# Order of four row products on TensorE in a gated scan kernel: value, gate, gate, value instead of value, gate, value, gate

## Chip, cores and metric

One core of one Trainium2 chip. The metric is the device time of the whole program in microseconds (us), the median of several executions. An execution's time is some 1.7 us above the span of its trace (from the first to the last instruction); both are used below, each under its name.

Engines in the profile: PE is TensorE, PEld its weight loads, DVE is VectorE, ACT is ScalarE, POOL is GpSimd, SP is SyncE.

## The reference, cut to what matters

```python
# x: 8 x 4224 x 192; a causal convolution of 7 taps, one set of weights per group of 24 channels
x = conv(x, softmax(weight))
proj = x @ w_in                       # 192 -> 1024
val, gate = proj[..., :512], proj[..., 512:]
a = exp(A_log)                        # one decay per channel of 512 in the kernel
for t in range(S):                    # along the sequence, per batch
    h = a * h + val[:, t]
    ys[:, t] = h
out = (gate * sigmoid(gate) * ys) @ w_out     # 512 -> 192
```

(The sequential part is a scan; the reference takes the decay as drawn, between 0 and 0.61.) The depth of `x @ w_in` is 192, which is 128 rows and 64 rows of the array. So each value or gate product needs a full product and a row product of 64 rows.

## The kernel before

The sequence is cut into blocks of 960 positions; a step is one block and one of four groups of 128 channels, 144 steps in all. A pass of the main loop does two steps, s and s+1, and has the work of four engines in flight: TensorE makes value, gate, output and convolution products; DVE scans the value; ACT makes SiLU of the gate; POOL multiplies the two.

```python
ps_v = ctx.enter_context(tc.tile_pool(name="ps_v", bufs=2, space=bass.MemoryType.PSUM))
ps_m = ctx.enter_context(tc.tile_pool(name="ps_m", bufs=2, space=bass.MemoryType.PSUM))
# ... (cut) two tiles each, of two banks a tile. ps_v holds values, ps_m everything else.

def proj(ps, s, gate, full, start):
    # ... (cut) two instructions, one for each half of the 960 columns
    for k in range(2):
        o = ps[:, BANK - w + k * w : BANK + k * w].rearrange("p (t m) -> p t m", m=M)
        if full:
            nc.tensor.matmul(o, w1[:, m], cols(xc, k * nh, nh), ...)          # 128 rows
        else:
            r = slice(k * P // 2, k * P // 2 + P // 2)
            nc.tensor.matmul(o, w2[r, m], cols(xc, 2 * nh, nh, r), ...)       # rows 0-63 or 64-127
# ...
for p in range(NP):
    s = 2 * p
    b = s // NC
    scan(s)                               # DVE, reads the value of s
    if p:
        val(s + 1, True, True)            # (step, full or row product, first of its sum)
    gate(s, True, True)
    val(s + 1, False, False)
    gate(s, False, False)
    val(s + 2, False, True)
    gate(s + 1, False, True)
    silu(s)                               # ACT
    mul(nc.gpsimd, s)                     # POOL
    # ... (loads)
    gate(s + 1, True, False)
    val(s + 2, True, False)
    silu(s + 1)
    if p < NP - 1:
        scan(s + 1)
        mul(nc.gpsimd, s + 1)
    # ... (loads)
    late = 0 if b >= NSB - 7 else 2
    if LEAD <= p < NP - 2 and done_step(u) < s - late:
        units(1)                          # sixteen output products; need POOL's product of done_step(u)
    # ... (transposes, convolution products of a later block)
```

Three things matter. The two row instructions of a pair use different halves of the array and run side by side (in the trace they start 3 ns apart). The value of step s+2 goes into the tile that the scan of step s reads, as there are only two. And an output unit needs a product of POOL that is at least three steps back, but from block 29 on (`late = 0`) only one.

## Time and profile before

| | before |
|---|---|
| median time | 332.81 us (3 runs, 332.68 to 332.9) |
| span of the trace | 331.5 us |
| busy share of the span: PE, DVE, POOL, ACT | 96, 94, 95, 80% |

The groups that carry three of the engines, from the page of the kernel before (line, engine, operation, output and inputs, shapes, count; then busy us and mean ns; then the idle time in front and what ended most of it):

```profile
L487 POOL TENSOR_TENSOR y<-sg,h 128x960 bf16<-128x960 bf16 (+3 forms) x159 | 279.7, 1789 | 5.2 <-ACT sg L449 4.3
L464 DVE TENSOR_TENSOR_SCAN h<-av,h,pv 128x960 bf16<-128x960 f32 (+5 forms) x140 | 265.9, 1937 | 6.3 <-issue 2.7
...
L429 PE MATMUL pv<-xc,w 64*128 64x480 bf16 (+2 forms) x288 | 53.8, 365 | 2.5 <-DVE h L464 1.6
```

POOL's products and DVE's scans fill the two engines nearly alone. The last line is the value's row products: PE stands before them and the scan ends the wait. That 1.6 us is far less than what the wait costs, since idle time is counted from the modelled end of the product before, 0.38 us after its start, while the next could have started after 0.20. For this wait one has to read starts.

### The profile page before, as it was taken

The page shows a single profiled execution, that of the slowest core. Times are in us where ns is not written, and L with a number is a line of the kernel's source. Part 1 is how long each engine was busy: PE and PEld are TensorE (multiplying, and loading weights), DVE is VectorE, ACT ScalarE, POOL GpSimd, SP SyncE. Part 2 cuts the span into 40 slices and gives each one's busy share as a digit, 9 for nine tenths or more (in the row PEclk, how much of TensorE's full clock was granted, in tenths as well). Part 3 has the DMA queues.
Part 4 walks back from the last instruction along what each step waited for, and adds up shares of the span by engine and source line. Part 5 has one row for each costly group of instructions (what it writes and reads, how often), then busy time and mean ns, then how long its engine had stood idle before and what let it go on. Part 6 is the DMA issues. An engine that isn't in the chain of part 4 may idle for free.

```text
span 331.5 us, 6839 instructions
## 1 busy us (share of the span) xinstructions
PE 318.4 (96%) x2593; PEld 191.3 (58%) x2593; DVE 310.0 (94%) x190; ACT 264.6 (80%) x449; POOL 313.9 (95%) x210
## 2 busy tenths in 40 slices
PE   8888899999999999999999999999999999999984
PEld 3544446666555666666555566666555666665554
DVE  3699999999999999999999999999999999999991
ACT  4588888888888888888888888888888888887663
POOL 5699999999999999999999999999999999989992
PEclk9999999999999999999999999999999999999998
DMA  7589699989989698959696989799998999653223
GB/s 164 57 91 104 71 132 227 169 185 161 220 140 239 126 224 141 218 126 222 146 202 172 145 222 143 202 153 228 135 245 114 200 191 184 130 155 122 96 98 142
DMA packets 99512, 53.40 MB, mean 161 GB/s; under 512 B 89915, under 2 KB 90967, under 8 KB 99479
## 3 DMA queue, kind: packets, MB, share of 16 engines
q1 hardware_dynamic: 58375, 38.93, 50.0%
q0 software_dynamic: 40560, 13.55, 39.0%
q10 hardware_dynamic: 544, 0.49, 0.5%
q8 instruction: 20, 0.33, 0.4%
q14 instruction: 13, 0.11, 0.1%
HBM read 28.46 MB, written 25.95 MB: 164 GB/s over the span
## 4 chain that ended last, share of the span: by engine, by line
PE 85%; DMA 5%; ACT 4%; POOL 2%; DVE 1%; issue 1%; DVEq 0%; ACTq 0%
PE pm L496 25%; PE pm L423 18%; PE pv L423 16%; PE pv L429 12%; PE pm L429 8%; PE pm L254 6%; ACT sg L449 2%; DMA w2r<-in_moe_w_in_dram 2%; DMA xb<-in_x_dram 2%; ACT xc L102 1%; DVE h L464 1%; DMA xr<-in_x_dram 1%; POOL y L487 1%; DMA out_dram<-osb 1%; ACT yc L102 0%
## 5 line engine op out<-in xcount | busy, mean ns | idle before, releaser
L487 POOL TENSOR_TENSOR y<-sg,h 128x960 bf16<-128x960 bf16 (+3 forms) x159 | 279.7, 1789 | 5.2 <-ACT sg L449 4.3
L464 DVE TENSOR_TENSOR_SCAN h<-av,h,pv 128x960 bf16<-128x960 f32 (+5 forms) x140 | 265.9, 1937 | 6.3 <-issue 2.7
L449 ACT ACTIVATE sg<-pm 128x960 bf16<-128x960 f32 (+2 forms) x144 | 135.9, 954 | 39.2 <-PE pm L429 32.2
L496 PEld LDWEIGHTS <-y 128*128 128x128 bf16 x1056 | 91.0, 114 | 13.1 <-POOL y L487 0.6
L496 PE MATMUL pm<-wout,y 128*128 128x192 bf16 x1056 | 97.8, 246 | 0.7 <-POOL y L487 0.4
L423 PEld LDWEIGHTS <-w 128*128 128x128 bf16 x576 | 48.9, 97 | 61.5 <-issue 33.1
L423 PE MATMUL pm<-xc,w 128*128 128x480 bf16 (+2 forms) x288 | 81.3, 364 | 2.0 <-ACT xc L102 1.3
L423 PE MATMUL pv<-xc,w 128*128 128x480 bf16 (+2 forms) x288 | 80.8, 361 | 0.6 <-DVE h L464 0.4
L102 ACT COPY osb<-pm 128x384 f32<-128x384 f32 x131 | 62.7, 479 | 15.5 <-PE pm L496 13.5
L102 ACT CAST yc<-pm 128x256 bf16<-128x256 f32 (+2 forms) x140 | 59.7, 491 | 2.6 <-PE pm L254 2.6
L429 PE MATMUL pv<-xc,w 64*128 64x480 bf16 (+2 forms) x288 | 53.8, 365 | 2.5 <-DVE h L464 1.6
L429 PEld LDWEIGHTS <-w 64*128 64x128 bf16 x576 | 23.3, 94 | 50.8 <-issue 37.9
L429 PE MATMUL pm<-xc,w 64*128 64x480 bf16 (+2 forms) x288 | 52.5, 358 | 0.0
L464 DVE TENSOR_TENSOR_SCAN h<-av,pv 128x720 bf16<-128x720 f32 (+4 forms) x32 | 42.4, 1330 | 2.0 <-PE pv L429 2.0
L254 PE MATMUL pm<-xb,tb 126*128 126x192 bf16 (+1 forms) x280 | 34.0, 244 | 1.4 <-ACT sg L449 0.7
L254 PEld LDWEIGHTS <-tb 126*128 126x128 bf16 x288 | 24.6, 97 | 3.3 <-DMA xb<-in_x_dram 1.5
L128 POOL DMA_DIRECT2D xb<-in_x_dram x21 | 25.5, 1214 | 0.1
L194 PE MATMUL pm<-wm 128*128 128x512 bf16 x24 | 7.7, 480 | 1.3 <-DVE wm L138 1.3
L102 ACT COPY xc<-pm 128x960 bf16<-128x960 bf16 (+2 forms) x9 | 6.1, 728 | 0.6 <-PE pm L375 0.5
L194 PEld LDWEIGHTS <-wm 128*128 128x128 bf16 x24 | 2.7, 119 | 4.9 <-issue 2.7
L394 POOL CAST w<-w1r 128x512 bf16<-128x512 f32 x2 | 1.2, 606 | 3.7 <-DMA xsf<-in_x_dram 3.7
L375 PEld LDWEIGHTS <-yc 120*128 120x128 bf16 x57 | 3.4, 98 | 1.3 <-ACT yc L102 0.6
(59 smaller groups left out, 30.2 us busy)
## 6 DMA issues: line engine op xcount, KB each, us to landing
out_dram<-osb SPq DMA_DIRECT2D x65, 384.0 KB
xb<-in_x_dram POOLq DMA_DIRECT2D x13, 756.0 KB, 12.4
xb<-in_x_dram POOLq DMA_DIRECT2D x7, 378.0 KB, 5.6
xb<-in_x_dram POOLq DMA_DIRECT2D x1, 519.8 KB, 9.8
xc<-yc SPq DMA_TRANSPOSE x31
w1r<-in_moe_w_in_dram SPq DMA_DIRECT2D x1, 448.0 KB
xr<-in_x_dram ACTq DMA_DIRECT2D x1, 283.5 KB
w2r<-in_moe_w_in_dram SPq DMA_DIRECT2D x2, 128.0 KB
```

Source lines behind the costliest of these rows:

```text
L102: return eng.copy(o, i) if eng is nc.scalar else eng.tensor_copy(o, i)
L128: nc.gpsimd.dma_start(xt[:, a0 : a0 + n, :], rows(FIRST[b0], n))
L194: nc.tensor.matmul(pw[:, 0:BANK], wm[:, 0:P], wm, start=True, stop=True)
L254: nc.tensor.matmul(pc[:, :, i * G : i * G + G], tb[:, h, :], xt[:, a0 : a0 + n, h * G : h * G + G], start=True, stop=True, skip_group_chec ...
L375: nc.tensor.transpose(pt[:, o + i * M : o + i * M + M], y[0:M, k * P : k * P + P], ident)
L394: nc.gpsimd.tensor_copy(w1[:, lo : lo + DI], w1r[:, lo : lo + DI])
L423: nc.tensor.matmul(o, w1[:, m], cols(xc, k * nh, nh), start=start, stop=not start, skip_group_check=True,)
L429: nc.tensor.matmul(o, w2[r, m], cols(xc, 2 * nh, nh, r), start=start, stop=not start, skip_group_check=True,)
L449: nc.scalar.activation(sg[:, 0 : 2 * w], pgs.pop(s)[:, BANK - w : BANK + w], Act.Silu)
L464: nc.vector.tensor_tensor_scan(h[:, lo:hi], av[:, c : c + 1].to_broadcast([P, hi - lo]), pv[:, BANK - w + lo : BANK - w + hi], initial=0.0 ...
L487: eng.tensor_mul(yr[c][:, ring(t0 + lo, hi - lo)], sg[:, lo:hi], h[:, lo:hi])
L496: nc.tensor.matmul(ps[:, o : o + D], yr[c][:, r.start + j : r.stop : UB], wout[:, c, :], start=(c == 0 and j % 2 == 0), stop=(c == NC - 1) ...
```

## The change

Its intent: the value of step s+2 is the one row product of the four that waits for a scan. Putting the gate's in front of it gives the scan one slot more. No product is added or removed.

```diff
         gate(s, True, True)
         val(s + 1, False, False)
         gate(s, False, False)
+        gate(s + 1, False, True)
         val(s + 2, False, True)
-        gate(s + 1, False, True)
         silu(s)
```

## The prediction

> **Names.** One pass of the main loop handles two steps. V1 and V2 are the value products of steps s+1 and s+2, G0 and G1 the gate products of s and s+1. Each consists of two full products (128 rows) and a pair of row products (64 rows each, the two running side by side). TensorE's order in a pass is: V1 full, G0 full, the four row pairs V1 G0 V2 G1, G1 full, V2 full, sixteen output products, four convolution products. The change makes the row pairs V1 G0 G1 V2.
>
> **What bounds the kernel now.** First the page: busy shares and the chain that ended last.
>
> ```profile
> PE 318.4 (96%) x2593; PEld 191.3 (58%) x2593; DVE 310.0 (94%) x190; ACT 264.6 (80%) x449; POOL 313.9 (95%) x210
> ...
> PE 85%; DMA 5%; ACT 4%; POOL 2%; DVE 1%; issue 1%; DVEq 0%; ACTq 0%
> ```
>
> Three engines are nearly full, so no share names the bound, and the chain names PE only because PE is followed whenever it shows no gap. So I went to the timeline of PE, start to start, over two passes (columns: start, time, engine, line, operation, tiles, shapes, count):
>
> ```profile
> 152.93 0.57 PE L423 MATMUL pv<-xc,w 128*128 128x480 bf16 x2
> ...
> 154.05 0.36 PE L429 MATMUL pm<-xc,w 64*128 64x480 bf16 x2
> 154.25 0.37 PE L429 MATMUL pv<-xc,w 64*128 64x480 bf16 x2
> ...
> 157.23 0.57 PE L423 MATMUL pv<-xc,w 128*128 128x480 bf16 x2
> ...
> 158.13 0.38 PE L429 MATMUL pv<-xc,w 64*128 64x480 bf16 x2
> 158.35 0.37 PE L429 MATMUL pm<-xc,w 64*128 64x480 bf16 x2
> 158.69 0.38 PE L429 MATMUL pv<-xc,w 64*128 64x480 bf16 x2
> 158.89 0.38 PE L429 MATMUL pm<-xc,w 64*128 64x480 bf16 x2
> ```
>
> The first pass takes 157.23 - 152.93 = 4.30 us and its row pairs start 0.20 apart. In the second, V2's pair starts 0.34 after G0's: PE stood for 0.14 us. Next pass starts at 161.67, so this one took 4.44. The scans say what it stood for:
>
> ```profile
> 152.00 2.19 DVE L464 TENSOR_TENSOR_SCAN h<-av,h,pv 128x960 bf16<-128x960 f32 x1
> ...
> 154.31 2.21 DVE L464 TENSOR_TENSOR_SCAN h<-av,h,pv 128x960 bf16<-128x960 f32 x1
> ...
> 156.44 2.19 DVE L464 TENSOR_TENSOR_SCAN h<-av,h,pv 128x960 bf16<-128x960 f32 x1
> ```
>
> The scan from 156.44 ends at 158.63 and V2's pair starts at 158.69: V2 needs the value buffer (two of them) that this scan reads. DVE stands too: the first scan ends at 154.19, the next starts at 154.31, because its V1 row pair only began at 153.84. Two engines wait for each other in turn. Third, POOL, by stretches (us, then PE, PEld, DVE, ACT, POOL busy), then at single gaps (idle before and what ended it in brackets), then PE's wait for it:
>
> ```profile
> 60.00:177.00 117.00, 116.55 (x958) 70.87 (x957) 115.40 (x67) 97.31 (x166) 116.85 (x70) 1.00 1.02 182
> 177.00:280.00 103.00, 102.42 (x843) 62.89 (x842) 101.45 (x56) 86.10 (x145) 100.53 (x60) 1.00 1.01 178
> ```
>
> ```profile
> 195.28 2.01 POOL L487 TENSOR_TENSOR y<-sg,h 128x960 bf16<-128x960 bf16 x1 [0.69 <-ACT sg L449]
> ...
> 212.80 2.01 POOL L487 TENSOR_TENSOR y<-sg,h 128x960 bf16<-128x960 bf16 x1 [0.43 <-ACT sg L449]
> ```
>
> ```profile
> 279.63 1.01 PE L496 MATMUL pm<-wout,y 128*128 128x192 bf16 x10 [0.40 <-POOL y L487]
> ```
>
> POOL is full to 177 us, working off a backlog: its product of step 15 starts 4.6 us after scan and SiLU are there, that of step 74 only 0.1 us after. Then small gaps appear. The last line shows PE waiting for POOL in pass 60, where the kernel's rule for emitting output units loosens and a unit needs the step just before.
>
> **What the Trainium skill says.** "TensorE: Matmul & The Clock Gate", Part 3, The mechanism: matrix products stay in program order, only weight loads are pulled ahead. The trace agrees: G1, whose inputs are there, starts 0.20 us behind V2 at 158.89, not before it. "TensorEngine Tiling (Array Packing)", Key Properties: changing the tiling mode drains the array. The trace agrees: the last row pair lasts 0.29 to 0.30 us to the next full product's start against 0.20 inside the group, and full to row costs as much. Both orders switch twice a pass, so this cost stays. "Perfetto Trace Analysis", Identifying the Most-Contended Engine: matmul busy time is a poor measure of PE and occupancy a good one for VectorE and GpSimd; here PE's 96% includes the stand of 0.14 us, so it agrees.
>
> **The change part by part.** Nothing is removed or added; DVE, ACT, POOL and SyncE keep their lists word for word. On PE two pairs change places, and V2's wait for the scan goes with it.
>
> *The loop it shortens.* Take it over two passes: scan end to V2's pair 0.06 us; V2's pair to the next pass's V1 pair 3.89 (V2 rows 0.20, G1 rows 0.31, G1 full 0.41, V2 full 0.41, output 1.32, convolution 0.33, V1 full 0.41, G0 full 0.50); V1's pair to the start of its scan 0.47; then two scans, 2.13 start to start plus 2.19. Sum 8.74 us, and the passes measure 4.30 + 4.44 = 8.74: this loop sets the pace. Moving G1's rows ahead of V2's takes one slot, 0.20, out of it: 8.54. PE's own work is twice 4.30 = 8.59, so now PE sets the pace, without V2 waiting, and two passes gain 0.15 us. In passes whose scan is cut at a sequence border the scans are 0.04 longer each; there some 0.03 of wait remains.
>
> *Sum over the run.* V2's slot over 0.20 adds up, in the timeline, to 2.02 us in 26 passes from 74 to 187 us, 0.48 in three to 200, 1.26 in 17 to 275, 0.04 in the first of the next seven: 3.8 us of PE time before pass 60. The 1.4 us before 74 follow mostly single late scans (0.59 at 57.98) that the order doesn't touch. After pass 60, six passes hold 0.47 us.
>
> *What POOL lets through.* POOL's continuous pace is 4.28 us a pass (steps 15 to 74, loads included) and PE's would be 4.30, so POOL keeps its backlog of about 4 us instead of losing it. It can win only its gaps: from 177 us to the product of step 119, which pass 60 needs, 2.4 us, of which 0.3 is a load behind a memset and likely stays. That product ended at 279.57 and should end near 277.4. PE would arrive at 278.57 - 3.8 = 274.8 and wait some 2.5 us for it. So of PE's 3.8 us some 2.0 pass through pass 60. Behind it POOL has no loads and runs at 3.95 a pass, faster than PE, so the rest is PE's and the scans': I allow 0.3 of the 0.47, as passes without convolution are bound by two scans, 4.26. Total 2.3 us: 332.8 - 2.3 = 330.5 us.
>
> **The rivals.** *Everything passes:* if POOL had no say, the 3.8 + 0.47 us would all show: 328.5 us. For: POOL's gaps after 177 show that it was waiting. Against: it has none in the 117 us before, and PE waits for it in pass 60. *G1 takes the wait:* G1 now comes 0.20 us earlier and needs a buffer that ACT is emptying:
>
> ```profile
> 153.17 0.93 ACT L102 CAST yc<-pm 128x256 bf16<-128x256 f32 x3
> ```
>
> These casts end at 154.10; with the 0.06 to 0.09 us that releases take here, G1 could start by 154.19, and its new place is 154.25. Margin 0.06 in passes with three casts, more in the others (one cast, end 158.28, place 158.55). If it fails, V2 stands behind it too: half the gain gone, 331.8 us. *Nothing moves:* scans are the true bound with 2 x 2.13 = 4.26 us a pass of 4.37; or POOL's first 177 us fix the end: 332.8 us. Against: DVE stands 0.04 to 0.13 us in each pass, and POOL's late gaps are real. *Output waits for SiLU:* the first output product needs SiLU(s), which ends 0.09 before it at 155.49 in the pass without a wait; that path is as long as PE's, unchanged by the order, and I give it little.
>
> **Range and chances.** The centre is 330.5 us. Most of the uncertainty is how many of POOL's gaps close and whether pass 60 swallows more: 329.3 if half of the held-back gain gets out, 332.2 if G1's wait or new gaps eat most of it. The three runs before spread only 0.22 us. Over 2% faster would be under 326.2, beyond even the first rival: 0.01. Over 2% slower has no mechanism here: 0.01. Within 2%: 0.98.
>
> **What would show it.** V2's slot excess gone (each pass near 4.30 us between 74 and 270 us); DVE's stand before the odd scans smaller or moved; POOL without gaps to step 119, its backlog near 4 us there; PE's wait for POOL in pass 60 grown from 0.6 to about 2.5 us; scans 3 to 4 us earlier at 270 us, but the end only some 2 us. I am wrong if a new wait stands before G1's row pair, if POOL's backlog empties all the same, or if the pace stays at 4.37.

## The result, and the profile after

| | before | after | ratio |
|---|---|---|---|
| first series | 332.75 us (4 runs) | 329.27 us (4 runs, 329.21 to 330.65) | 0.9907 (0.988 to 0.9933) |
| second series, on one chip | 332.65 us (11 runs) | 329.80 us (6 runs, 329.15 to 330.79) | 0.9917 (0.9894 to 0.994) |

A ratio is the mean time of one kernel's runs over that of the other's runs of the same rounds, with its 95% interval, so not quite the ratio of the medians beside it. The gain is 0.8 to 0.9%: 2.9 to 3.5 us by the medians.

The page of the changed kernel, busy shares and chain:

```profile
PE 314.1 (96%) x2593; PEld 198.3 (61%) x2593; DVE 308.7 (94%) x190; ACT 262.5 (80%) x449; POOL 313.4 (96%) x210
...
PE 82%; DMA 5%; ACT 4%; POOL 4%; DVE 2%; issue 1%; DVEq 0%; ACTq 0%; POOLq 0%
```

Busy shares hardly move and would not have told anything. What moved is in the timeline of PE, here one pass and the start of the next:

```profile
154.70 0.57 PE L423 MATMUL pv<-xc,w 128*128 128x480 bf16 x2
155.11 0.57 PE L423 MATMUL pm<-xc,w 128*128 128x480 bf16 x2
155.61 0.38 PE L429 MATMUL pv<-xc,w 64*128 64x480 bf16 x2
155.82 0.57 PE L429 MATMUL pm<-xc,w 64*128 64x480 bf16 x4
156.22 0.37 PE L429 MATMUL pv<-xc,w 64*128 64x480 bf16 x2
156.52 0.58 PE L423 MATMUL pm<-xc,w 128*128 128x480 bf16 x2
...
159.00 0.57 PE L423 MATMUL pv<-xc,w 128*128 128x480 bf16 x2
```

The two gate pairs are one row now (four instructions in the same tile pool). V2 starts at 156.22, 0.40 after the first of them, two slots of 0.20, and the pass takes 159.00 - 154.70 = 4.30 us. So does the next, which begins at 159.00 and ends at 163.29. The pass of 4.44 us is gone. In the 26 passes between 74 and 187 us the stands of V2 added up to 2.02 us before. Now, from pass 12 to 66, the slot before V2 exceeds 0.20 only at the sequence borders, by 0.02, and once at a late scan, by 0.29 (the pass from 184.81).

DVE and POOL by stretches (us, then busy PE, PEld, DVE, ACT, POOL); the first fence is the kernel before, in a stretch that the prediction did not show, the second the changed one:

```profile
177.00:264.00 87.00, 86.82 (x716) 53.49 (x715) 85.65 (x48) 73.12 (x124) 85.25 (x50) 1.00 1.02 175
```

```profile
60.00:177.00 117.00, 116.81 (x976) 75.69 (x974) 116.99 (x67) 98.72 (x171) 116.87 (x70) 1.00 1.02 183
177.00:264.00 87.00, 86.87 (x727) 56.44 (x728) 86.66 (x50) 73.19 (x126) 86.89 (x50) 1.00 0.95 183
```

POOL stood for 1.75 us of these 87 us; now it stands for 0.11. DVE, which stood 1.60 us in the 117 us before, has no gap left there, but it is not full by its own work: its scans now start 2.13 and 2.17 us after one another in turn, 4.30 us for two, PE's pace.

Then pass 60 of the changed kernel, the output products:

```profile
273.77 0.49 PE L496 MATMUL pm<-wout,y 128*128 128x192 bf16 x4
...
274.67 0.36 PE L496 MATMUL pm<-wout,y 128*128 128x192 bf16 x2 [0.41 <-POOL y L487]
...
276.61 1.01 PE L496 MATMUL pm<-wout,y 128*128 128x192 bf16 x10 [1.59 <-POOL y L487]
...
277.46 0.49 PE L254 MATMUL pm<-xb,tb 126*128 126x192 bf16 x4
```

Four products run, then two, then ten: each group needs POOL's product of one more step, and the last group starts when that of step 119 is there. The sixteen take 3.70 us to the start of the next row instead of 1.32, a wait of 2.38 us. Before it was 0.59.

By stretches, with the start of each pass taken from PE's timeline:

| stretch of the span | before, us | after, us | gained |
|---|---|---|---|
| start to pass 7 | 42.46 | 42.02 | 0.44 |
| passes 7 to 11 | 22.88 | 22.38 | 0.50 |
| passes 12 to 59 | 210.53 | 206.72 | 3.81 |
| pass 60 | 4.94 | 6.68 | -1.74 |
| passes 61 to 66 | 25.97 | 25.45 | 0.52 |
| pass 67 to the end | 24.68 | 24.33 | 0.35 |
| span | 331.46 | 327.58 | 3.88 |

The first row is for the most part not the order's: POOL's first product started at 15.66 and 15.13 us, and what it waits for (the weights' transfer and cast) lies ahead of every product that moved. In the other runs that start lies between 14.7 and 15.7 us, below 15.0 with both orders. Pass 7 began between 41.6 and 42.5 us with the orders that wait and between 41.4 and 42.0 with the changed one (runs with chained scan pieces left out), so a small part of the 0.44 may be the order's; no run separates it.

### The profile page after: what moved, and what is told of

Read it like the earlier page. It is cut to its first block, busy times and chain, and to the rows that moved or that the text cites. A ratio compares the mean times of both kernels' runs of the same rounds, so it can differ in the third digit from the quotient of the medians.

```text
span 327.6 us, 6839 instructions
## 1 busy us (share of the span) xinstructions
PE 314.1 (96%) x2593; PEld 198.3 (61%) x2593; DVE 308.7 (94%) x190; ACT 262.5 (80%) x449; POOL 313.4 (96%) x210
## 4 chain that ended last, share of the span: by engine, by line
PE 82%; DMA 5%; ACT 4%; POOL 4%; DVE 2%; issue 1%; DVEq 0%; ACTq 0%; POOLq 0%
PE pm L496 25%; PE pm L423 18%; PE pv L423 15%; PE pv L429 11%; PE pm L429 7%; PE pm L254 6%; POOL y L487 3%; ACT sg L449 2%; DVE h L464 2%; DMA xb<-in_x_dram 2%; DMA w2r<-in_moe_w_in_dram 2%; ACT xc L102 1%; DMA xr<-in_x_dram 1%; DMA out_dram<-osb 1%; ACT yc L102 0%
## 5 line engine op out<-in xcount | busy, mean ns | idle before, releaser
L449 ACT ACTIVATE sg<-pm 128x960 bf16<-128x960 f32 (+2 forms) x144 | 133.9, 954 | 36.1 <-PE pm L429 31.5
L429 PEld LDWEIGHTS <-w 64*128 64x128 bf16 x576 | 30.4, 94 | 47.5 <-issue 31.3
L429 PE MATMUL pm<-xc,w 64*128 64x480 bf16 (+2 forms) x288 | 40.6, 358 | 0.5 <-ACT xc L102 0.5
```

The costliest lines, as they stand in the source:

```text
L429: nc.tensor.matmul(o, w2[r, m], cols(xc, 2 * nh, nh, r), start=start, stop=not start, skip_group_check=True,)
L449: nc.scalar.activation(sg[:, 0 : 2 * w], pgs.pop(s)[:, BANK - w : BANK + w], Act.Silu)
```

## The experiments

V1, V2, G0, G1 are the row pairs as in the prediction. For the pace I give the time of passes 12 to 59 from each trace, as in the table.

### Where V1 and V2 stand

If the way from V2's pair to the next pass's V1 pair sets the pace, then V1 counts as much as V2. Two more orders test it: one with V2 last but V1 late, one with V2 third and V1 late.

```diff
-        val(s + 1, False, False)
         gate(s, False, False)
+        val(s + 1, False, False)
         gate(s + 1, False, True)
         val(s + 2, False, True)
```

> Row pairs in the order G0 V1 G1 V2: V2 stays last as in the changed kernel, but V1 comes one slot (0.20 us) later. Loop theory (the way from V2's pair to the next V1's pair and two scans set the pace): that way is 3.89 us again as in the kernel before, so 8.74 us for two passes, 4.37 a pass; V2 waits for the scan again; 332.8 us (332.2 to 333.4). Rival 'V2 only has to be last': 329.3 us, passes of 4.30. Rival 'two gate products side by side run better on the array': no adjacent gates here, 332.8 us too, but then without a wait of V2 and with longer slots of the row pairs.

Measured: 331.99 us, ratio 0.9978 (0.9946 to 1.0009). Passes 12 to 59 took 210.44 us, against 210.53 of the kernel before. In its timeline V2 waits just as before, though it is last:

```profile
157.72 0.37 PE L429 MATMUL pv<-xc,w 64*128 64x480 bf16 x2
157.93 0.36 PE L429 MATMUL pm<-xc,w 64*128 64x480 bf16 x2
158.26 0.38 PE L429 MATMUL pv<-xc,w 64*128 64x480 bf16 x2
```

V2 starts 0.33 after G1 instead of 0.20. The time is 0.2 us below the band that I gave, the pace is right to a tenth of a microsecond. "V2 only has to be last" falls. The rival of the adjacent gates named the same time, but with longer slots and without a wait of V2; the slots are 0.20 as ever and the wait is there.

```diff
-        val(s + 1, False, False)
         gate(s, False, False)
-        gate(s + 1, False, True)
+        val(s + 1, False, False)
         val(s + 2, False, True)
+        gate(s + 1, False, True)
```

(against the changed kernel)

> Row pairs in the order G0 V1 V2 G1: V2 third as in the kernel before, V1 one slot later. Loop theory: the way from V2 to the next V1 grows to 4.09 us, the loop to 8.94, 4.47 us a pass, 0.10 more than before in some 53 passes less the wait in pass 60: 337.5 us (336.5 to 338.5), slower than both kernels. Rival 'only V2's place in the group counts': 332.8 us. Rival 'like products side by side run better': 329.3 us.

Measured: 338.22 us, ratio 1.0174 (1.0145 to 1.0203). Passes 12 to 59 took 215.19 us, 4.48 each, where 4.47 was expected:

```profile
106.48 0.37 PE L429 MATMUL pv<-xc,w 64*128 64x480 bf16 x2
107.01 0.38 PE L429 MATMUL pv<-xc,w 64*128 64x480 bf16 x2 [0.17 <-DVE h L464]
107.22 0.38 PE L429 MATMUL pm<-xc,w 64*128 64x480 bf16 x2
```

V2 stands 0.53 after V1, a wait of 0.33, twice and more that of the kernel before. Four orders of the same instructions, and only the number of slots from V2 to the next V1 tells their pace: one less is 206.7 us, the same is 210.5 and 210.4, one more is 215.2. Both rivals fall with this one, as they expected no loss.

### Longer scans, first attempt

A loop through two scans must answer to their length. Every uncut scan was cut in two, in both orders.

```diff
-        ends = sorted(set([0] + cuts + [n]))
+        ends = sorted(set([0] + cuts + [n] + ([] if cuts else [n // 3])))
```

> The kernel before, with every uncut scan cut into two (a third and two thirds), which makes a scan some 0.04 us longer; result unchanged. Loop theory: 8.74 + 0.09 = 8.83 for two passes, 4.41 a pass, 0.044 more in some 53 passes, part of it taken from the wait in pass 60: 335 us (334 to 335.8). Rival 'TensorE's own work sets the pace in both orders': at most the tail's half microsecond, 333.3 us.

> The changed kernel with the same cut of the scans. Loop theory: 8.54 + 0.09 = 8.63 against TensorE's 8.59: 4.315 a pass, some 1 us more by pass 60, which shrinks the wait for POOL there from 2.4 to about 1.4 us and so doesn't reach the end; some 0.5 us in the last passes, where the scans follow each other: 329.8 us (329.3 to 330.5). Rival 'the scans set the pace in both orders': the same loss as in the kernel before with cut scans, 331.5 us.

Measured: 349.75 us (ratio 1.0513) and 347.86 us (ratio 1.0457). Both expectations missed by far, because the size of the lever was wrong: the second piece starts from the last element of the first and waits for it (the second attempt, below, differs in that alone). Five pieces, two and a half scans, in the trace of the changed order:

```profile
199.99 5.56 DVE L464 TENSOR_TENSOR_SCAN h<-av,h,pv 128x320 bf16<-128x320 f32 x5
```

In the steady part two scans took 4.71 us, 2.35 each instead of 2.13, so 0.22 more and not 0.04. Twice 2.35 is above any loop or PE's work, DVE sets the pace alone, and PE waits 0.40 for it in each pass, in both orders (passes of 4.71 us in both traces, shorter only where a scan was cut at a border already). So this pair tells only that the order is worth little (1.9 us here) once the scans are the bound; it does not part the theories.

### Longer scans, second attempt

The second piece now starts from zero, as pieces at a sequence border do, and so waits for nothing.

```diff
+        cuts = cuts or [n // 3]
         ends = sorted(set([0] + cuts + [n]))
```

> The kernel before, every scan cut in two whose second piece starts from zero instead of from the first piece's end (the result is wrong on purpose); so the second piece waits for nothing, as at the cuts that the kernel has already, where two passes measured 4.34 + 4.49 = 8.83 us. Loop theory: 4.41 a pass all along, 0.043 more in some 43 passes up to pass 60, of which 0.6 is taken from the wait there, and 0.3 behind it: 334.3 us (333.6 to 335.2). Rival 'TensorE's own work sets the pace in both orders': 332.8 us.

> The changed kernel with the same cut from zero (wrong result on purpose). Two scans take 2 x 2.174 = 4.35 us, the loop 8.63 for two passes, TensorE 4.30 a pass: the scans set 4.35, 0.05 more in some 43 passes, 2.1 us by pass 60, which the wait of 2.4 us for POOL there swallows; 0.5 us behind it: 329.9 us (329.4 to 330.8). So the distance between the orders grows to over 4 us. Rival 'the order's gain doesn't depend on the scans': the same distance as without cuts, 3 us.

Measured: 333.93 us for the kernel before (ratio 1.0035, 1.0023 to 1.0047) and 329.85 us for the changed one (ratio 0.9915, 0.9896 to 0.9935). I had announced a wrong result, but the comparison with the reference passed. That fits a decay of at most 0.61, with which what is dropped at a cut vanishes within some positions. The two timelines of PE, first the order before, then the changed one:

```profile
149.62 0.37 PE L429 MATMUL pm<-xc,w 64*128 64x480 bf16 x2
150.04 0.38 PE L429 MATMUL pv<-xc,w 64*128 64x480 bf16 x2
```

```profile
147.61 0.57 PE L429 MATMUL pm<-xc,w 64*128 64x480 bf16 x4
148.04 0.38 PE L429 MATMUL pv<-xc,w 64*128 64x480 bf16 x2
```

Before, V2's wait grew from 0.14 to 0.22 us in every second pass, and passes 12 to 59 took 211.99 us, 1.46 more. In the changed order it is 0.02 (0.43 for two slots) and the passes took 207.13, 0.41 more; the wait in pass 60 fell from 2.4 to 2.0 us. The times are as expected. The pace of the changed order is better than I wrote: 4.315 us a pass, PE's and the loop's, not the 4.35 of two scans, so scans of this form don't need the 2.174 us that I had taken for their least. The distance between the orders in passes 12 to 59 grew from 3.81 us to 4.86, that of the medians from 2.9 to 3.5 (the two series) to 4.1: the gain does depend on the scans.

### The wait for POOL in pass 60

First the changed kernel again, to see what repeats:

> The changed kernel once more, for its ratio to the kernel before with a narrower interval and a second profile: ratio 0.989 (0.9885 to 0.9905), wait in pass 60 of 2.2 to 2.5 us, passes of 4.297 us. If the 0.5 us by which its weights arrived earlier in the first profile was chance, the second profile may show it gone.

Measured: 329.80 us, ratio 0.9917, a little above the band. Passes 12 to 59 took 206.74 us (206.72 in the first trace). The sixteen products of pass 60 took 3.94 us, a wait of 2.62, more than I gave. POOL's first product started at 15.28 us here, between 15.66 of the kernel before and 15.13 of the first trace, so there part of the luck is gone; PE, however, began pass 7 at 41.85 us, 0.17 earlier than in the first trace.

Is this wait what keeps the rest of the gain? Taking work from POOL should tell. In both orders the product of step 118 went to DVE:

```diff
-        mul(nc.gpsimd, s)
+        if s != 118:
+            mul(nc.gpsimd, s)
         # ...
             scan(s + 1)
+            if s == 118:
+                mul(nc.vector, s)
             mul(nc.gpsimd, s + 1)
```

> The changed kernel with one of POOL's 144 products, that of step 118, moved to DVE behind the scan of step 119. POOL-cap theory (of TensorE's saved time, 2.4 us are given back in pass 60, waiting for POOL's product of step 119): POOL gets there 2.0 us earlier, the wait falls from 2.4 to about 0.4 us or, as DVE and with it TensorE lose some 0.7 us to the product, to nothing; the end comes 1.0 to 1.6 us earlier, 328.0 us (327.5 to 328.5). Rival 'the wait in pass 60 is slack and the end is set by something else': 329.3 us or, by DVE's added work, 330 us.

> The same move in the kernel before. POOL-cap theory: TensorE waits only 0.6 us for POOL in pass 60 here and loses up to 0.7 us to DVE's product: 332.8 us (332.3 to 333.3), no gain. Rival 'POOL's total work sets the end of this kernel too': 331 us.

Measured: 333.54 us (ratio 1.003) and 336.44 us (ratio 1.0112, with runs from 334.4 to 338.7). Both are some 4 us slower than the same order without the move. The trace of the changed order shows why, first DVE and POOL:

```profile
270.05 4.90 DVE L487 TENSOR_TENSOR y<-sg,h 128x960 bf16<-128x960 bf16 x1
274.87 4.30 DVE L464 TENSOR_TENSOR_SCAN h<-av,h,pv 128x960 bf16<-128x960 f32 x2
```

```profile
268.51 5.91 POOL L487 TENSOR_TENSOR y<-sg,h 128x960 bf16<-128x960 bf16 x3
277.21 2.00 POOL L487 TENSOR_TENSOR y<-sg,h 128x960 bf16<-128x960 bf16 x1 [2.79 <-DVE h L464]
```

The product took 4.90 us on DVE, and it ended at 274.94, 0.51 us after POOL's three products that ran in a row from 268.51 to 274.43. In the order before, it took 3.13 us and ended 0.51 us after a product of POOL likewise. The Trainium skill knows this: "SBUF — State Buffer", Who interferes with whom, says that a DVE instruction with two SBUF inputs contends with a GpSimd instruction that reads SBUF; its summary rules for kernel authors add that the one that issues second is held up entirely. I had not looked there. The trace agrees, and goes further: it was held up through the rest of one POOL product and two more. (No run has this product on DVE while POOL is idle, so the cause of the hold rests on these two traces and the page.)

The stall had a second cost, on PE:

```profile
277.12 0.58 PE L429 MATMUL pv<-xc,w 64*128 64x480 bf16 x2 [4.60 <-DVE h L464]
...
279.21 2.50 PE L496 MATMUL pm<-wout,y 128*128 128x192 bf16 x16
281.55 0.50 PE L254 MATMUL pm<-xb,tb 126*128 126x192 bf16 x4
```

V2 stood some 4.8 us, and when PE went on its granted clock was 0.50 (`--windows`, 276 to 281 us): the sixteen output products took 2.34 us to the next row instead of 1.32, and the pass from V2 on 4.76 instead of 2.78. Together with the 2.4 us of waiting for POOL that went away, this is the growth of pass 60 from 6.68 to 11.05 us. In the order before PE stood 3.1 us and the granted clock was 0.50 from 281 to 286 us; the one run of it with a granted clock of 1.0 over the span is the fastest (334.39 us). In both traces of the changed kernel itself the granted clock stays at 1.00 through the wait of 2.4 to 2.6 us in pass 60. Its three slower runs of ten (330.65, 330.70 and 330.79 us) have a mean granted clock of 0.994, the others 0.997 or more; they were not traced, so whether that wait cost them the clock is not shown.

So this experiment put a stall into the loop and says nothing of the cap. The product of step 118 was then left out instead, which takes the work from POOL and gives it to nobody:

```diff
-        mul(nc.gpsimd, s)
+        if s != 118:
+            mul(nc.gpsimd, s)
```

> The changed kernel without POOL's product of step 118 (wrong result on purpose: the output reads what the ring held), which takes 2.0 us from POOL and adds nothing elsewhere. POOL-cap theory: the wait in pass 60 falls from 2.4 to 0.4 us and the end comes 2.0 us earlier: ratio to the kernel before 0.985, 327.6 us (327.2 to 328.3). Rival 'the wait in pass 60 is slack': 329.6 us.

> The kernel before without POOL's product of step 118 (wrong result on purpose). POOL-cap theory: TensorE waits only 0.6 us for POOL here, and that is all there is to win: 332.2 us (331.9 to 332.8), ratio 0.998. Rival 'POOL's total work sets the end of the kernel before': 2.0 us earlier, 330.7 us.

Measured: 327.60 us for the changed order (ratio 0.9841, 0.9829 to 0.9854) and 331.90 us for the order before (ratio 0.9969, 0.9957 to 0.9981). Their outputs are wrong, which doesn't matter for the times. Pass 60 of the changed order:

```profile
273.50 0.66 PE L496 MATMUL pm<-wout,y 128*128 128x192 bf16 x6
274.52 1.01 PE L496 MATMUL pm<-wout,y 128*128 128x192 bf16 x10 [0.36 <-POOL y L487]
```

The sixteen take 1.87 us to the next row, a wait of 0.55. Against the changed order in the other series, pass 60 is 1.8 to 2.1 us shorter and the median 1.7 to 2.2 us lower; the order before had only 0.6 us to win (its wait is gone, 1.32 us for the sixteen); its median fell by 1.05, and the interval of its ratio, 0.6 to 1.4 us, begins at what was expected. In its trace pass 60 is 0.59 us shorter. So 2.0 us of POOL's work are worth all of that in the changed kernel and much less in the kernel before: POOL caps the changed kernel at pass 60.

The other way to the same question is to leave POOL alone and take away the unit that waits:

```diff
-        late = 0 if b >= NSB - 7 else 2
+        late = 2
         # ...
-    assert u >= NU - 3, u
+    assert u >= NU - 4, u
```

> The changed kernel without the loosened rule: an output unit always needs a step at least three back, so pass 60 emits none and one unit more is left for the end. POOL-cap theory: the wait in pass 60 goes; 2.4 + 1.3 us earlier in pass 61, one unit more (1.3 us) at the end: 328.2 us (327.3 to 329.0). Rival 'POOL itself sets the end, whatever waits for it': 330.5 us, the unit's 1.3 us added and nothing won.

Measured: 327.79 us, result correct, ratio 0.9855 (0.9826 to 0.9884) to the kernel before, while the changed kernel in the same rounds had 0.9917 (0.9894 to 0.994). Around pass 60 it goes from the value products to the convolution at once:

```profile
272.70 0.57 PE L423 MATMUL pv<-xc,w 128*128 128x480 bf16 x2
273.11 0.49 PE L254 MATMUL pm<-xb,tb 126*128 126x192 bf16 x4
274.11 0.56 PE L423 MATMUL pv<-xc,w 128*128 128x480 bf16 x2 [0.51 <-DVE h L464]
```

Pass 60 took 3.65 us, 3.0 to 3.3 less than with the wait. Of that, passes 61 to 66 give back 0.6 us (V2 waits for a scan again in pass 61, as PE has run ahead of the scans), and the stretch from pass 67 to the end 1.4 (one unit more). So 1.1 to 1.3 us remain. The medians differ by 2.0; in this trace the other 0.7 us is the part before pass 12, which was over that much earlier and which the edit doesn't touch. This version beats both kernels.

## Why the prediction was right or wrong

The centre was 330.5 us with a range from 329.3 to 332.2. The two series gave 329.27 and 329.80 us: one on the lower edge of the range, one inside, both within 2% of the kernel before, as given.

*The loop it shortens:* right. 8.74 us for two passes became 2 x 4.30, PE's own pace, without a wait of V2. The four orders have the pace that their way from V2 to V1 gives, and longer scans cost the order before 1.46 us where they cost the changed one 0.41.

*Sum over the run, before pass 60:* right in its main term, 3.8 us expected and 3.81 measured in passes 12 to 59. That they agree to a hundredth is luck: of V2's stand in these passes (3.84 us, 0.13 of it in pass 13, which the prediction did not count here) 0.38 stayed; what made up for it is the step from the last row pair to the next full product, 0.298 us where V2 hasn't waited against 0.312 where it has. The part on the time before 74 us failed: "mostly single late scans that the order doesn't touch". The order does touch them. In passes 7, 9 and 11 V2 waited 0.50, 0.23 and 0.56 us and waits 0.30, 0.12 and 0.35 now: against a late scan, too, V2 has one slot more. That is 0.50 us in passes 7 to 11 (0.29 in the second trace of the changed kernel).

*What POOL lets through:* right. PE arrives early in pass 60 and waits there: 2.5 us expected, 2.38 and 2.62 measured. The closeness is partly luck, for the 2.5 does not follow from the prediction's own two times: PE at 274.8 and the product's end at 277.4 are 2.6 us apart, and in the kernel before a distance of 1.00 us made a wait of 0.59, so that some 2.2 would follow. PE came at 273.77 and the product ended at 276.56, both about 1 us earlier than given. POOL's backlog at step 119 was 4.1 us, near the 4 that the prediction named as a sign (2.5 before). The product of step 119 had ended at 279.57 in the kernel before. Of the 3.01 us, 0.53 is the start by chance, 2.00 are gaps closed between step 0 and pass 60 (2.30 us before, 0.31 left: the load behind a memset, as expected), and 0.47 is that its products from step 60 on take less time end to end when they follow each other without gaps, which I had not counted. The two runs that take the cap away (without a product, without the unit) win what it held.

*Behind pass 60:* mis-sized. I allowed 0.3 us, of the 0.47 that six passes hold, and nothing after them; it was 0.52 in those six, 61 to 66, and 0.35 from pass 67 on. Only the last of the six has no convolution, so the reason for the discount hardly applied to them. Later passes are bound by the scans there, but the wait for them was longer than two scans' 4.26 us need: 4.39 us in the pass from 306.78 before, 4.24 in the same pass after.

*The rivals:* "everything passes" (328.5 us) fell by pass 60. "G1 takes the wait" fell: G1 starts 0.20 us behind G0 in every pass from 12 to 59. "Nothing moves" fell. "Output waits for SiLU" did not show: the value products before the output keep their 0.40 us.

What stays open: why single scans come 0.3 to 0.6 us late. They come in both kernels, near passes 11 and 40, and what the profile names in front of them ("issue", or a product of POOL that had long been done) doesn't explain it.

## What to carry to other kernels

Where two engines wait for each other in turn, busy shares and idle sums need not show it, and here did not: write down the loop, from one wait through the work of both engines back to the same wait, and compare its sum with the measured pace. Then an instruction's place in a queue can be worth one slot in each turn of the loop, whether or not it is the one that waits: here a turn is two passes, and moving V1, which doesn't wait, cost 0.19 us in two (215.19 against 210.53 us in 48 passes). Before counting the gain, look for the next engine that is nearly full and for the place where the first one needs it, as the saved time can be given back there in a single wait.

## What the Trainium skill lacked or had wrong

- "Perfetto Trace Analysis", Identifying the Most-Contended Engine, names the engine with the highest occupancy as the one to improve (TensorE is judged by MFU and the share of weight loads instead). Here PE, DVE and POOL stood at 96, 94 and 95%, and the pace of 8.74 us for two passes was that of none of them but of a loop through PE and DVE; PE's own work was 8.59. The page lacks the case of a loop.
- "SBUF — State Buffer", Who interferes with whom, is right that a DVE instruction with two SBUF inputs is held up by POOL, and its summary rules say until the first finishes. Here it was held up over POOL instructions that follow each other without a gap: 4.90 us, until 0.51 us after POOL's row ended. The page doesn't say that a queue of them can keep the pair.
- No page says what it costs that a scan starts from the last element of the scan in front of it: 2.35 us for a scan in two chained pieces against 2.13 us in one; pieces that start from a constant cost at most 0.04 us.
